# Expert kernel on one core: the fifth batch's routing steps, expert 1's banks and its weight splits in another order

## The chip, the cores and the metric

The kernel runs on one core of a Trainium2 chip. The metric is the device time of one launch in microseconds. All times in this document are microseconds unless another unit stands beside them. TensorE, VectorE (DVE), ScalarE (ACT) and GpSimd (POOL) each work through a queue of their own in order; SyncE (SP) issues most of the DMAs, GpSimd issues the indirect ones (gathers and scatters of rows by index).

## The reference: what is computed

First a linear attention with decay: for 4 batches, 8 heads, 768 positions and 64 features, `state = gamma * state + k v^T` and `y = q state / 8`. The result, seen as 3072 tokens of 512 features, goes through a two-level mixture of experts. `x @ w_group` chooses one of 4 groups, `x @ w_expert[g]` one of 4 experts in it, so each token goes to one of 16 experts:

```python
h  = np.maximum(x[tokens] @ w1[g, e], 0.0)     # 512 -> 1024
ye = h @ w2[g, e]                              # 1024 -> 512
out[tokens] = (g_w * e_w)[:, None] * ye        # two softmax weights
```

The weights and tokens are float32. Each product is made of three 16-bit products: a value is split into a high and a low half (`wh`, `wl` for weights, `xbh`, `xbl` for tokens, `hh`, `hl` for the hidden layer), and high x high, high x low and low x high are summed in PSUM.

## The kernel before

**Attention, steps 0 to 11.** A step `i` handles two blocks of 128 positions for all heads: scores, mask, value products, state, then the logits of the step before (`logits_mm`, L319), the transposes of its output to rows in DRAM (`trans_mm`, L345, into `xd`), and the selection of its 20 logits per token into the PSUM bank `log` (`select_mm`, L332). In some steps the selection is left to the next step (`select_late`).

**Routing, batches 0 to 5.** Two steps make a batch of 4 blocks. `route(b)` is a generator whose pieces are dealt out between the steps (`route_steps`): the choice of group and expert (L384 to L402), which gives a one-hot `oh`; then, after a "wait", the ranks by six matmuls into `log` (L435, L437), the place of each token in its expert's list (L443 to L452, then `places` on GpSimd, L475 to L477), and after one more "wait" the softmax sums and the token's weight (`weights`, L412 to L425 on DVE, L428 to L431 on GpSimd, which cut the weight into three 16-bit pieces). Before the change the sums of all batches but the last are written to the bank `log`. A read or write of that bank waits for those before it, whatever the columns. To put a batch into the lists, DVE makes a mask of list segments (`chosen`, L493) and a one-hot of the places (`marks`, L484), GpSimd multiplies the mask by the pieces (`entries`, L500), and TensorE sums one-hot x product over the blocks (`tally`, L521); DVE adds the sums to the lists (L528).

**The hand-over.** Expert 0 is worked on first. Its first 128 tokens (`ua`) come from the first four batches, so its two layers (`layers`, L839 and L874) run while batches 4 and 5 are still being routed: `first(n)` runs `n` pieces of them (a piece is half of a hidden block, 12 matmuls; eight pieces are the first layer). Expert 0's other tokens (`ub`, up to 108) need the late lists: `late_entries`, `late_marks` (L554) and `late_ids` (L562, L566) make their indices directly, `gather` (L774) fetches the rows. The column count of `ub` (`late_count`, L573 and L574) is loaded into a register of TensorE (`shape`, L806), which cuts its matmuls to the tokens that are there. After that the tally of batches 4 and 5 closes all lists, `order` sorts the experts by size, and `counts` makes their column counts (L638 to L644).

**The experts.** `va` is expert 1, `us[1]` and so on the others in order of size. For each expert eight splits of its weights are made: ACT makes `wh` (L750), DVE makes `wl` (L752), each a piece of 128x1024. A load of 1 MB (`wload`, L724) brings two pieces, and four buffers hold the loads, so that a load waits until the two splits of an older one are done. Tokens are transposed by TensorE (`xtrans`, L792), ACT makes `xbh` (L794) and DVE `xbl` (L817). The hidden layer is made in four blocks (L839), each in a PSUM bank that ACT (`hh`, L844) and DVE (`hl`, L847) read; for `ua` and `ub` three of them are of the tag "big" and the fourth is "tra". Then comes the second layer: L946 for `ub`, L921 and L924 for experts with up to 256 tokens, L874 for full blocks of tokens. While expert `j` runs, `fill(k)` deals out the splits and transposes of expert `j + 1` and the loads of expert `j + 2`. All instructions are issued in the order in which the program writes them, engine by engine. The lines around the loop over `layers(ub)` before the change:

```python
for i, k in enumerate(self.layers(ub)):
    if i in (1, 3, 5, 7, 13, 15):
        low = (1, 3, 5, 7, 13, 15).index(i) + 2
        self.wsplit(va, low, high=False)
        if low % 2:
            self.wload(us[1], low // 2)
    if i in (8, 10):
        self.xtrans(va, ("tra", "sta")[i // 2 - 4], (i // 2 - 4,))
    if i == 11:
        self.counts()
```

Here `i` counts the pieces of `ub`: 0 to 7 are its first layer (after every odd one a hidden block is done), 8 to 15 the eight parts of its second.

Of the kernel before, what the change touches and what calls it, by code (L numbers as in the profile page):

```python
# [22 lines left out]
P = 128  # L23
# [41 lines left out]
BM = 4  # L65
# [41 lines left out]
class Kernel:  # L107
# [251 lines left out]
    def route(self, i):  # L359
# [5 lines left out]
        cst = self.rest  # L365

        def t(name, *shape, dt=F32):
            return rp.tile([P, BM] + list(shape), dt, name=name)[:, 0:n]

        def ps(a, *shape):  # L370
            v = self.log[:, a:a + n * int(np.prod(shape))]
# [4 lines left out]
        L5, d, q, eo = ps(LG, 5, 4), ps(LD, 5, 4), ps(LQ, 5, 4), ps(LO, 4, 4)  # L376
        r1, sm, se, w = ps(LR, NX), ps(LS, 5), ps(LS + 20, 1)[:, :, 0], ps(LS + 24, 1)[:, :, 0]
        sf, pc = self.sf[:, c0:c0 + n], self.pc[:, c0:c0 + n]
        if c0 + n == NCH:
            sm, se, w = t("sms", 5), t("ses"), t("ws")  # L380
        desc = cst[:, C_DESC:C_DESC + 20].rearrange("p (g e) -> p g e", g=5).unsqueeze(1).broadcast_to([P, n, 5, 4])
        oh = self.oh[:, BM - n:BM + 1]
# [685 lines left out]
    def attention(self, extra, beside):  # L1068
# [27 lines left out]
        for i in range(NS2):  # L1096
            last = i == NS2 - 1
            if i == 10:
                self.route_steps(99, True)
                self.spread(3)  # L1100
            if not last:
                self.vprep(i + 1)
            beside(i, -1)
            if i + 1 < NC:
                self.decay_next(i + 1)
            beside(i, 0)
            if i:
                if i > 2:
                    self.outs(i)
                if i > 1:  # L1110
                    scores(i + 1, 0)
                if i % 2 and not last:
                    self.select_late()
                if i in (5, 7, 9):
                    self.tally()
                if i > 2:
                    self.state_out(i, 0)
                if last:
                    self.select_late()
                if i > 1:  # L1120
                    self.state_out(i, 1)
                self.select_late()
                if i % 2 == 0:
                    self.route_steps(99, True)
                if i > 1:
                    scores(i + 1, 1)
            self.load("q", i + 3)
            self.load("v", i + 3)
            if i % 2:
                self.route_steps(99)  # L1130
            beside(i, 2)
            if i:
                self.value_out(i, 0)
            self.value_out(i, 1)
            if i:
                self.state_mm(i, 0)
            self.state_mm(i, 1)
            self.state_copy(i)
            if i == 10:
                self.tally()  # L1140
                beside(i, 5)
            beside(i, 4)
            if i:
                self.logits_mm(i - 1, 1 if last or i % NC == NC - 2 or i + 1 in KEYED else 2)
            self.out_x(i)
            if i < 2:
                scores(i + 1, 0)
                scores(i + 1, 1)
            if i in (4, 6, 8):
                self.spread(i // 2 - 2)  # L1150
            if last:
                self.route_steps(1, True)
            beside(i, 1)
            if not last:
                banks = (self.log, self.sh[0]) if i < 2 else None
                if i == 0:
                    self.keys_mm(1, (0,), banks)
                    self.outs(1)
                    self.state_out(1, 0)
                    self.state_out(1, 1)  # L1160
                    self.keys_mm(1, (1,), banks)
                else:
                    self.keys_mm(i + 1, banks=banks)
                if i == 1:
                    self.outs(2)
                    self.state_out(2, 0)
                self.load("k", i + 4)
            if i:
                late = i + 1 in KEYED or i % NC == NC - 2
                self.trans_mm(i - 1, late=late)  # L1170
                if late:
                    self.late = i - 1
                else:
                    del self.st[i - 1]
            beside(i, 3)
            if last:
                self.route_steps(99)
            if i % 2:
                self.route_steps(99, True)
            if i == 1:  # L1180
                self.const_pieces()
            if last:
                extra(i)
            if i and i % 2 == 0:
                self.steps.append(self.route(i // 2 - 1))
            if not last:
                extra(i)
# [15 lines left out]
    def run(self):  # L1203
        tc, nc = self.tc, self.nc
        with ExitStack() as ctx:
# [80 lines left out]
            last = NS2 - 1  # L1286
            self.logits_mm(last)
            self.trans_mm(last, self.yp)
            nc.gpsimd.memset(self.xg[1], 0.0)
            self.wsplit(va, 1, low=False)  # L1290
            for k in range(8, 16):
                self.wload_part(va, k)
            assert not self.steps
            route = self.route(len(BATCHES) - 1)
            while next(route) != "wait":
                pass
            self.held = []
            first(3)
            self.wsplit(va, 2, low=False)
            late = [self.late_entries(5, self.oh[:, 0:BM, 0:1])]  # L1300
            next(route)
            p, y = self.at
            hot = self.marks(p)
            ent, sel = self.chosen(y)
            late.insert(0, self.late_entries(4, sel[:, :, 1:2]))
            self.spreads.append((hot, self.entries(4, ent, sel)))
            while next(route) != "late":
                pass
            first(2)
            ub["mt"] = self.pairs()  # L1310
            self.late_ids(ub["mt"], (hot, late[0]), (self.hot, late[1]))
            self.gather(ub)
# [7 lines left out]
            self.spreads.append((self.marks(p, self.yp), ent))  # L1320
            nc.vector.scalar_tensor_tensor(*self.held[3])
            self.held = None
            self.late_count()
            self.wsplit(va, 3, low=False)
            self.steps.append(self.order())
            self.route_steps(5)
            for i, k in enumerate(self.first):
                if i == 0:
                    self.shape(ub, 5, 0, self.late_cols)
                    self.wsplit(va, 4, low=False)  # L1330
                if i == 1:
                    self.tally("sta")
                    fin = self.final.rearrange("p e i w -> p (e i) w")
                    self.tokens(fin[:, :, 0], fin[:, :, 1], self.lists)
# [10 lines left out]
            for u in us[1:3]:  # L1345
                self.listed(u)
            self.own_counts()
            for k in range(2):
                self.wsplit(va, k, high=False)
            self.wload(us[1], 0)  # L1350
            ub["wh"], ub["wl"] = ua["wh"], ua["wl"]
            self.gather(us[1])
            for i, k in enumerate(self.layers(ub)):
                if i in (1, 3):
                    self.wsplit(va, 6 + i // 2, low=False)
                if i in (1, 3, 5, 7, 13, 15):
                    low = (1, 3, 5, 7, 13, 15).index(i) + 2
                    self.wsplit(va, low, high=False)
                    if low % 2:
                        self.wload(us[1], low // 2)  # L1360
                if i in (8, 10):
                    self.xtrans(va, ("tra", "sta")[i // 2 - 4], (i // 2 - 4,))
                if i in (9, 10):
                    self.shape(va, 0, i - 9, cols(0, i - 9))
                if i == 11:
                    self.counts()
            self.rp = self.rp2
            self.steps.append(self.items())
# [2 lines left out]
            for j, u in enumerate(us):  # L1371
# [4 lines left out]
                def fill(k):  # L1376
                    if k == 0:
                        self.ytrans(pv)
                    if nx is not None and k in (1, 2):
                        self.shape(nx, (j + 1) % 2, k - 1, cols(j + 1, k - 1))  # L1380
                    if nx is not None and k in KX:
# [64 lines left out]
```

## Time and profile before

| | |
|---|---|
| time, median of 3 runs (lowest, highest) | 412.25 (411.23, 412.8) |
| the profiled execution: its time, its span | 414.38, 412.7 |
| TensorE busy, share of the span | 393.7, 95% |
| DVE, ACT, GpSimd busy | 71%, 54%, 40% |
| mean granted clock of TensorE | 0.992 |
| HBM read, written | 94.18 MB, 13.20 MB |

The span is the time from the first to the last instruction of one profiled execution; 1.68 of its time lie outside the span. Positions such as "at 128.5" are from the span's start. Attention ends and the experts begin at about 108, the loop over the experts begins at 138.3, and TensorE's last matmuls end near 405. In rows of a timeline the columns are: start, duration, engine, line, operation, output and inputs, shape, count, and in brackets the idle time of that engine before the instruction, with what ended it by the profile. That name is inferred from semaphore events.

### The profile page before, as it was taken

Reading aid. Unit: us, or ns where it says so; the run is one execution under the profiler, and the core shown is the slowest. Engines: PE = TensorE matmul, PEld = TensorE weight load, DVE = VectorE, ACT = ScalarE, POOL = GpSimd, SP = SyncE. Lnnn points to the kernel's source line nnn. Section 1 sums busy time; section 2 is a strip of 40 time slices with the busy share of each in tenths; the row PEclk is TensorE's granted clock in tenths of the full one; section 3 lists DMA queues with packets and bytes.
Section 4 is the critical chain, followed back from the end, with each engine's and each line's share of the span. In section 5 each row is a group of like instructions: output and inputs, shape, how many; then the busy total and the mean of one; then the engine's idle time right before and its main releaser. Section 6 shows DMA issues by size and latency. Waiting matters only on the chain.

```text
span 412.7 us, 13870 instructions
## 1 busy us (share of the span) xinstructions
PE 393.7 (95%) x5809; PEld 326.9 (79%) x5841; DVE 293.4 (71%) x483; ACT 223.1 (54%) x340; POOL 165.2 (40%) x172
## 2 busy tenths in 40 slices
PE   9999999989886999999999999999999999999992
PEld 5889989868656979586879797887978879878792
DVE  3575776867769687896767686877869778688620
ACT  2324435534644456555556566666766667667620
POOL 4532767759564205241506051542514415142001
PEclk9999999999999999999999999999999999999998
DMA  7999999975846866777787877879788898797001
GB/s 264 371 335 325 312 352 319 310 273 176 269 153 209 342 228 245 236 262 248 251 252 253 295 249 284 281 273 303 278 306 282 299 317 299 253 341 266 6 35 35
DMA packets 39507, 107.13 MB, mean 260 GB/s; under 512 B 12116, under 2 KB 12244, under 8 KB 32276
## 3 DMA queue, kind: packets, MB, share of 16 engines
q1 hardware_dynamic: 29760, 93.57, 66.0%
q0 software_dynamic: 9536, 12.63, 8.9%
q8 instruction: 47, 0.77, 0.7%
q14 instruction: 16, 0.13, 0.1%
q10 hardware_dynamic: 148, 0.03, 0.0%
HBM read 94.18 MB, written 13.20 MB: 260 GB/s over the span
## 4 chain that ended last, share of the span: by engine, by line
PE 45%; issue 35%; POOL 10%; DVE 6%; ACT 1%; DMA 1%; POOLq 0%; SPq 0%; DVEq 0%; ACTq 0%
PE hps L839 10%; POOL out L998 6%; PE yps L874 6%; PE op L299 5%; PE sh L235 5%; POOL xg L774 4%; PE yps L921 3%; PE op L286 2%; PE stp L261 2%; PE sh L345 2%; PE yps L924 2%; PE tpx L792 1%; PE sh L220 1%; PE log L332 1%; PE yps L946 1%
## 5 line engine op out<-in xcount | busy, mean ns | idle before, releaser
L752 DVE TENSOR_TENSOR wl<-wf,wh 128x1024 bf16<-128x1024 f32 x120 | 145.3, 1220 | 37.7 <-ACT wh L750 36.7
L750 ACT ACTIVATE wh<-wf 128x1024 f16<-128x1024 f32 (+1 forms) x136 | 133.6, 1002 | 0.0
L839 PE MATMUL hps<-xbl,wh 128*128 128x128 f16 (+16 forms) x544 | 128.6, 249 | 0.0
L839 PE MATMUL hps<-xbh,wl 128*128 128x0 bf16 x544 | 125.8, 241 | 0.0
L839 PE MATMUL hps<-xbh,wh 128*128 128x0 bf16 x544 | 125.8, 241 | 0.0
L998 POOL DMA_INDIRECT out<-yo,mt x30 | 39.3, 1309 | 162.9 <-ACT yo L980 125.0
L839 PEld LDWEIGHTS <-wh 128*128 128x128 f16 x1088 | 94.9, 98 | 1.0 <-issue 0.2
L924 PEld LDWEIGHTS <-wh 128*128 128x128 f16 x768 | 47.1, 97 | 22.9
L844 ACT ACTIVATE hh<-hps 128x256 bf16<-128x256 f32 (+16 forms) x68 | 34.2, 503 | 44.2 <-PE hps L839 42.4
L774 POOL DMA_INDIRECT xg<-xd,mt x30 | 51.1, 1704 | 15.2 <-issue 4.9
L839 PEld LDWEIGHTS <-wl 128*128 128x128 bf16 x544 | 53.2, 98 | 0.7
L247 DVE TENSOR_TENSOR pf<-sh,tri 128x512 f32<-128x512 f32 x48 | 30.6, 685 | 24.8 <-PE sh L235 8.6
L794 ACT ACTIVATE xbh<-tpx 128x512 bf16<-128x512 f32 (+14 forms) x32 | 16.7, 523 | 52.4 <-PE tpx L792 52.4
L847 DVE SCALAR_TENSOR_TENSOR hl<-hps,hh 128x216 f16<-128x216 f32 (+15 forms) x64 | 36.7, 574 | 4.9 <-ACT hh L844 4.6
L921 PE MATMUL yps<-wh,hh 128*128 128x512 f16 x96 | 36.4, 379 | 0.0
L921 PE MATMUL yps<-wh,hl 128*128 128x512 f16 x96 | 36.4, 379 | 0.0
L921 PE MATMUL yps<-wl,hh 128*128 128x512 bf16 x96 | 36.3, 378 | 0.0
L817 DVE TENSOR_TENSOR xbl<-tpx,xbh 128x512 f16<-128x512 f32 (+14 forms) x32 | 19.1, 598 | 21.9 <-ACT xbh L794 21.5
L924 PEld LDWEIGHTS <-wl 128*128 128x128 bf16 x384 | 24.2, 97 | 11.4
L192 POOL TENSOR_TENSOR vs<-lv,cst 128x512 f32<-128x512 f32 x24 | 24.6, 1044 | 15.3 <-DMA lv<-qkv 8.8
L924 PE MATMUL yps<-hl,wh 128*128 128x108 f16 (+11 forms) x384 | 29.1, 198 | 0.0
L924 PE MATMUL yps<-hh,wh 128*128 128x0 bf16 x384 | 26.6, 190 | 0.0
(194 smaller groups left out, 601.9 us busy)
## 6 DMA issues: line engine op xcount, KB each, us to landing
wf<-w1p SPq DMA_DIRECT2D x28, 1024.0 KB
wf<-w2p SPq DMA_DIRECT2D x28, 1024.0 KB
lq<-qkv SPq DMA_DIRECT2D x24, 256.0 KB
lk<-qkv SPq DMA_DIRECT2D x24, 256.0 KB
lv<-qkv SPq DMA_DIRECT2D x24, 256.0 KB
xd<-xr SPq DMA_DIRECT2D x22, 256.0 KB
wf<-w1p SPq DMA_DIRECT2D x16, 256.0 KB
wf<-w2p SPq DMA_DIRECT2D x16, 256.0 KB
```

Of the source, the lines that this page charges most:

```text
L192: self.nc.gpsimd.tensor_tensor(o, v, g, ALU.mult)
L247: nc.vector.tensor_tensor(o, sc, tri, ALU.mult)
L750: nc.scalar.activation(u["wh"][i][:, cs], u["wf"][i][:, cs], AF.Copy)
L752: (eng or nc.vector).tensor_tensor(u["wl"][i][:, cs], u["wf"][i][:, cs], u["wh"][i][:, cs], ALU.subtract)
L774: nc.gpsimd.indirect_dma_start(out=xg[0:r, i, :], out_offset=None, in_=self.xd[0:n, :], in_offset=bass.IndirectOffsetOnAxis(ap=mt[0:r, i, ...
L839: nc.tensor.matmul(o, l[:, k, fs], m, start=(n == 0), stop=(n == 11), skip_group_check=True)
L844: nc.scalar.activation(hh[:, f, 0:W], hv[:, :, 0:W], AF.Relu)
L847: nc.vector.scalar_tensor_tensor(*rest)
L874: nc.tensor.matmul(ps[0:r, :], l[:, k, ts], m[k], start=(n == 0), stop=(n == 23))
L921: nc.tensor.matmul(big, h[:, k, 0:P], w[k], start=(n == 0), stop=(n == 23))
L924: nc.tensor.matmul(o, w[k][:, d * P:d * P + P], m, start=(n == 0 and d == 0), stop=(n == 23), skip_group_check=True,)
L998: s = nc.gpsimd.indirect_dma_start(out=self.out, out_offset=bass.IndirectOffsetOnAxis(ap=mt[0:r, i, 0:1].bitcast(U32), axis=0), in_=yo[0:r ...
```

## The change

It does six things. The selection of step 8's logits in step 10 goes behind the value and state matmuls. Batch 4's sums go to SBUF, as the last batch's do, with two buffers for `ex` and `go`. Batch 4's ranks are read in step 11 at once, its mask, one-hot and late product are made before the choice of the last batch, its sums after that choice, and its list product after the last batch's places. Of expert 0's first layer 2, 3 and 3 pieces are dealt out instead of 3, 2 and 3; the late column count and its register load move (the count ahead, the load behind). Expert 1's token transposes go to the banks "sta" and "big". Its `wl` splits and the loads of the next expert are dealt out over more pieces, the last two splits and the last load in expert 1's own first layer, and the column counts come after piece 15, not 11.

```diff
-            return rp.tile([P, BM] + list(shape), dt, name=name)[:, 0:n]
+            bufs = 2 if name in ("ex", "go") else 1
+            return rp.tile([P, BM] + list(shape), dt, name=name, bufs=bufs)[:, 0:n]
...
-        if c0 + n == NCH:
+        if c0 + n > NCH - 2 * BM + 1:
             sm, se, w = t("sms", 5), t("ses"), t("ws")
...
                 if i > 1:
                     self.state_out(i, 1)
-                self.select_late()
+                if i < NS2 - 2:
+                    self.select_late()
...
             if i == 10:
+                self.select_late()
                 self.tally()
...
             if last:
                 self.route_steps(1, True)
+                self.route_steps(99)
...
-            if last:
-                self.route_steps(99)
-            if i % 2:
+            if i % 2 and not last:
                 self.route_steps(99, True)
...
             self.trans_mm(last, self.yp)
-            nc.gpsimd.memset(self.xg[1], 0.0)
+            p, y = self.at
+            ent, sel = self.chosen(y)
+            hot = self.marks(p)
+            late = [self.late_entries(4, sel[:, :, 1:2])]
             self.wsplit(va, 1, low=False)
             for k in range(8, 16):
                 self.wload_part(va, k)
-            assert not self.steps
             route = self.route(len(BATCHES) - 1)
             while next(route) != "wait":
                 pass
             self.held = []
-            first(3)
+            self.route_steps(99, True)
+            assert not self.steps
+            first(2)
             self.wsplit(va, 2, low=False)
-            late = [self.late_entries(5, self.oh[:, 0:BM, 0:1])]
+            late.append(self.late_entries(5, self.oh[:, 0:BM, 0:1]))
             next(route)
-            p, y = self.at
-            hot = self.marks(p)
-            ent, sel = self.chosen(y)
-            late.insert(0, self.late_entries(4, sel[:, :, 1:2]))
-            self.spreads.append((hot, self.entries(4, ent, sel)))
             while next(route) != "late":
                 pass
-            first(2)
+            self.spreads.append((hot, self.entries(4, ent, sel)))
+            self.late_count()
+            first(3)
             ub["mt"] = self.pairs()
             self.late_ids(ub["mt"], (hot, late[0]), (self.hot, late[1]))
             self.gather(ub)
...
-            self.late_count()
+            nc.gpsimd.memset(self.xg[1], 0.0)
             self.wsplit(va, 3, low=False)
...
                 if i == 0:
-                    self.shape(ub, 5, 0, self.late_cols)
                     self.wsplit(va, 4, low=False)
                 if i == 1:
+                    self.shape(ub, 5, 0, self.late_cols)
                     self.tally("sta")
...
-            for k in range(2):
-                self.wsplit(va, k, high=False)
-            self.wload(us[1], 0)
+            self.wsplit(va, 0, high=False)
...
-                if i in (1, 3, 5, 7, 13, 15):
-                    low = (1, 3, 5, 7, 13, 15).index(i) + 2
+                if i in (3, 7, 9, 11, 13):
+                    low = (3, 7, 9, 11, 13).index(i) + 1
                     self.wsplit(va, low, high=False)
                     if low % 2:
                         self.wload(us[1], low // 2)
                 if i in (8, 10):
-                    self.xtrans(va, ("tra", "sta")[i // 2 - 4], (i // 2 - 4,))
+                    self.xtrans(va, ("sta", "big")[i // 2 - 4], (i // 2 - 4,))
...
-                if i == 11:
+                if i == 15:
                     self.counts()
...
+                    if j == 0 and k in (1, 2):
+                        self.wsplit(u, 5 + k, high=False)
+                        if k == 2:
+                            self.wload(nx, 3)
```

## Rows read from the trace of the kernel before

**Rows 1.** Busy time by stage: stretch, length, busy time (instructions) per engine, clock, DMA, GB/s.

```profile
113.00:120.00 7.00, 4.89 (x53) 3.30 (x55) 5.30 (x22) 3.60 (x5) 5.24 (x10) 1.00 0.69 242
...
132.20:138.30 6.10, 6.10 (x94) 6.01 (x97) 3.79 (x8) 1.13 (x2) 2.57 (x3) 0.72 1.01 410
...
160.00:200.00 40.00, 40.00 (x295) 29.14 (x298) 33.81 (x43) 23.06 (x30) 13.20 (x9) 1.00 0.77 257
```

**Rows 2.** TensorE's waits, 92 to 160: line, waited for, total, times, longest.

```profile
PE log L332 <- DVE ecols L463: 0.9, 1, 0.9
PE log L562 <- DVE lhot L554: 0.8, 1, 0.8
PE log L332 <- DVE wt L425: 0.7, 1, 0.7
PE log L435 <- ACT ex L408: 0.3, 1, 0.3
```

**Rows 3.** Timeline of DVE, 124 to 160.

```profile
125.20 2.34 DVE L752 TENSOR_TENSOR wl<-wf,wh 128x1024 bf16<-128x1024 f32 x2
...
131.75 0.36 DVE L847 SCALAR_TENSOR_TENSOR hl<-hps,hh 128x216 f16<-128x216 f32 x1
...
133.60 0.69 DVE L817 TENSOR_TENSOR xbl<-tpx,xbh 128x512 f16<-128x512 f32 x1 [0.36 <-issue]
...
136.66 0.41 DVE L638 TENSOR_TENSOR eqc<-eq,cnt 128x256 f32<-128x256 f32 x1
```

**Rows 4.** Timeline of TensorE, 126 to 142.

```profile
132.16 0.77 PE L792 MATMUL tpx<-ident,xg 128*128 128x128 f32 x4 [3.62 <-DVE hl L847]
```

**Rows 5.** Timeline of TensorE, 114 to 140.

```profile
118.65 0.38 PE L874 MATMUL yps<-wh,hh 128*128 128x512 f16 x1 [1.42 <-DVE gt L606]
...
119.94 0.72 PE L521 MATMUL tally<-yT,hot 128*128 128x160 bf16 x8
```

**Rows 6.** Timeline of ACT, 120 to 160.

```profile
127.28 0.83 ACT L844 ACTIVATE hh<-hps 128x216 bf16<-128x216 f32 x2
...
155.49 1.05 ACT L750 ACTIVATE wh<-wf 128x1024 f16<-128x1024 f32 x1
```

**Rows 7.** Timeline of DVE, 107 to 120.

```profile
106.84 0.23 DVE L412 TENSOR_REDUCE log<-ex 128x20 f32<-128x80 f32 x1
...
108.00 0.18 DVE L425 RECIPROCAL wt<-log 128x4 f32<-128x4 f32 x1
108.96 0.24 DVE L384 TENSOR_REDUCE m<-log 128x20 f32<-128x80 f32 x1 [0.78 <-PE log L332]
...
110.55 0.22 DVE L402 TENSOR_TENSOR oh<-log,go 128x64 bf16<-128x64 f32 x1
110.69 0.68 DVE L484 TENSOR_TENSOR hot<-rest,place 128x512 bf16<-128x512 f32 x1
...
112.56 1.07 DVE L554 SCALAR_TENSOR_TENSOR lhot<-rest,sf 128x512 bf16<-128x512 f32 x1 [0.18 <-DMA wf<-w2p]
...
117.56 0.14 DVE L574 TENSOR_SCALAR lcols<-fcols 1x1 int32<-1x1 f32 x1
```

**Rows 8.** Timeline of GpSimd, 107 to 120.

```profile
108.27 0.24 POOL L428 TENSOR_SCALAR pc<-wt 128x4 bf16<-128x4 f32 x1 [0.42 <-DVE wt L425]
...
109.20 0.21 POOL L431 TENSOR_TENSOR pc<-wt,pc 128x4 bf16<-128x4 f32 x1
...
111.81 1.27 POOL L500 TENSOR_TENSOR yT<-yT,pc 128x640 bf16<-128x640 bf16 x1
113.17 0.56 POOL L475 TENSOR_SCALAR tile<-sf 128x4 f32<-128x4 f32 x1
...
115.21 1.15 POOL L774 DMA_INDIRECT xg<-xd,mt  x1 [0.88 <-DMA wf<-w2p]
...
118.20 1.54 POOL L500 TENSOR_TENSOR yT<-yT,pc 128x640 bf16<-128x640 bf16 x1
```

**Rows 9.** Timeline of SP's DMA issues, 120 to 160.

```profile
133.37 7.32 SPq L724 DMA_DIRECT2D wf<-w2p  x2
```

## The prediction

> **What bounds the kernel now.** I read in this order: the busy time by stage, TensorE's waits, the timeline of each engine in the stretch that holds them. By stage, TensorE is busy for all of 160 to 200 at full clock [rows 1]; its waits from 160 on are none, so the expert loop is TensorE's own work, and this change leaves that work as it is (the same matmuls, transposes and splits in another order). What can be won lies before 160, in the list of TensorE's waits from 92 on: 0.9, 0.8, 0.7 and 0.3 us around the routing of the last two batches [rows 2], and two longer ones that the timeline shows in their place: 3.62 us before the transposes of expert 1's tokens (L792) [rows 4], 1.42 us before a second-layer matmul (L874) [rows 5]. They sum to 7.7 us. They cost more or less than they look. After the 3.62 us the granted clock is 0.72 on the mean over 132.2 to 138.3 [rows 1]: TensorE was busy for all 6.10 us, so 0.28 x 6.10 = 1.71 us went to the half-rate clock (1.2 of 2.4 GHz). And the small waits lie on a chain that runs through GpSimd, so that taking one away can open the next.
>
> **Part 1: expert 1's banks and the order of its splits** (the loop over layers(ub)). Before, DVE's queue there is two splits (125.20, 2.34 us), then in turn one hl (0.36 us) and one more split (1.20 us) [rows 3]: the fourth hl starts at 131.75 and ends at 132.11, when three more splits stood ahead of it. The first transposes of expert 1 go into the bank "tra", which holds the fourth hidden block until that hl has read it, so TensorE stands from 128.54 to 132.16 [rows 4]. The change sends the first transposes to "sta" and the second to "big". "sta" was last used by the tally (matmuls at 119.94 [rows 5], its sum on DVE right behind), "big" by the hidden block whose hl is the first in the queue. So the 3.62 us go, and with them the half-rate clock, 1.71 us.
>
> What is late next is DVE, since expert 1's first matmul needs both xl parts. New queue from 125.20: split 0, hl, hl, split 1, hl, hl, split 2, xl, split 3, xl. That is 4 x 1.20 + 4 x 0.36 + 2 x 0.69 = 7.6 us, to 132.8. hh, which hl waits for, is done for all four blocks by 128.11 [rows 6], so nothing holds the last two hl. TensorE is there at 128.54 + 6.10 x 0.72 = 132.9 (the busy time of the stretch at full clock). Both meet within 0.2 us: expert 1's matmuls start at 132.9, not at 138.29 or so: 5.4 us. If DVE starts late by x, x is lost; I allow 0 to 0.9.
>
> Of what is moved: the column counts (four instructions from 136.66, about 1.3 us [rows 3]) now come after splits 4 and 5, so at 132.8 + 2.4 + 1.3 = 136.5; TensorE wants them after expert 1's second hidden block, 4.8 us into it, at 137.7; cover 1.2 us. A register load from a fresh value held TensorE from 117.70 (the end of L574 [rows 7]) to 118.65 [rows 5], 0.95 us, so 0.25 us of cover is left and I charge nothing, 0.5 at worst. The last two splits (2 x 1.23) now stand in expert 1's own first layer; they are wanted in its second layer 9 us later, beside a DVE that is not full there. The fourth load of the next expert is issued after the last split and behind the first load of the expert after; the ACT split that reads it starts at 155.49 [rows 6], so at 150 in the new time. It is issued at about 143.3; 6.7 us for it, a charge of nothing in the sum and a rival below.
>
> **Part 2: the fifth batch.** Sums in SBUF for batch 4 too: the last selection (L332) no longer waits for the sums in the logit bank, 0.67 us [rows 2]. The late column count: the 1.4 us before L874 are TensorE's register load of it; DVE makes it at 117.56 behind all else [rows 7]; in the new order it is made right after the last one-hot, some 4 us earlier, and that wait goes. But the tally comes next on TensorE, right at 119.94, and it needs the last list product of GpSimd, 118.20 + 1.54 = 119.74 [rows 8]. So what counts is GpSimd's chain. New: selection ends 0.67 us earlier; the seven instructions of the choice from L384 (108.96) to the end of L402 (110.77) take 1.81, so the one-hot is there at 110.1 [rows 7]. Ahead of L384 batch 4's mask and one-hot (of which L484, 0.68 us, is the long one) take the place of its sums (106.84 to 108.18, 1.34 us), so L384 still waits for TensorE alone; behind the choice those sums now stand: reciprocal at 111.4. GpSimd: the four piece instructions 108.27 to 109.41 = 1.14 us, to 112.6; a small product 0.3; the three of the places, 0.84 when free and 1.16 beside DVE (L475 took 0.56 beside the last one-hot, 0.24 is the four-column rate of L428 [rows 8]), to 113.9; the list product of batch 4 with 1.27 to 1.54, to 115.2 to 115.5; the gather start, 115.21 before, now 115.3 to 116.2 (0.1 to the 0.88 us of idle that stood before it), 1.15 us long; the four pieces of batch 5, 1.14 to 1.73; the last product, 1.27 to 1.54. End: 118.9 to 120.6 against 119.74. I take the middle, 119.75: part 2 is worth **0**, bounds -0.85 to +0.9. TensorE has 11.02 - 0.26 - 0.84 - 1.42 = 8.5 us of work from the selection's end (108.92) to the tally; from 108.25, with 0.8 before the ranks (it has two half blocks there, not three) and 0.2 before the late ids, it comes to the tally at 117.8 and stands for some 1.9 us: the removed waits come back as one. The two buffers for ex and go only let batch 5 write them before batch 4's sums have read theirs. The memset of xg moves behind the last product (0.95 us of GpSimd, while it waited 1.8 us for the list before): nothing.
>
> The rule that speaks against this part is in the Trainium skill, SBUF — State Buffer, "Who interferes with whom": VectorE and GpSimd share one pair of ports as an exclusive lock, and the one that comes second stands until the first is done. L475 shows it: 0.56 us, ending at 113.73, 0.10 after the one-hot of DVE (112.56 + 1.07 [rows 7]). By it more of GpSimd's work would now fall on DVE's instructions with two SBUF operands, the moved sums among them, and the time would be that of the port rival below.
>
> **Part 3: the selection in step 10** goes behind the value matmuls; 0.9 us of TensorE's wait for the sums of batch 3 go [rows 2]. Behind it stands the gather of the first expert's tokens, which sits on GpSimd behind two scalings of v that do not move; its rows had just landed when TensorE transposed them. I take 0 to 0.6, value 0.1, and what comes of it runs into the chain of part 2.
>
> **The sum**, against the profiled execution: 414.38 - 3.62 - 1.71 (part 1) - 0 (part 2) - 0.1 (part 3) = 408.95, 5.4 less. The runs shown have a median of 412.25, 2.1 below the profiled one; I take the difference over unchanged: 412.25 - 5.4 = **406.8**. The likeliest case alone: best 405.3 (0.85 of part 2 and 0.6 of part 3 more), worst 408.6 (0.9 of each of parts 1 and 2 less).
>
> **Rivals.** (a) The clock. The half rate is lost again elsewhere: 1.9 us at the tally, 0.8 before the ranks and 0.2 before the late ids lie within ten us. For: it fell after an idle piece of 3.62 us. Against: 113 to 120, with the waits of 0.8 and 1.4, kept clock 1.00 [rows 1]. Or the timed runs did not all have it, and the median loses less. Either way 1.71 us: 408.5. 18%.
>
> (b) The port. DVE's sums of batch 5 stand behind GpSimd's product of batch 4 (1.27 us), the last marks behind its pieces; the last product ends 0.7 later: 407.5. 10%.
>
> (c) The change does not do what it says: the transposes in "sta" go, but the matmuls behind them wait for hl or xl as long, because DVE is full from 125.20 to 133.24 before [rows 3] and has the same work after. For: DVE has no pause there that would take up a shift. Against: four of its splits move behind the last xl. It needs DVE to be 3.5 us later than summed: 410.3 to 412.3. 7%.
>
> (d) The slower one: the next expert's weights. Loads 1, 2 and 3 are issued 1.8, 1.9 and 2.9 us later than now (load 2 at 133.37, load 3 at the end of that 7.32 us, 140.35 [rows 9]), while ACT wants them 5.4 us earlier. ACT runs in order, so a split without its weights holds the next hidden block. It decides from 6.7 us between issue and landing of load 3. All the rows say is that load 3 was there at 155.49, at most 15.1 us after its issue. At that bound ACT stands 15.1 - 6.7 = 8.4 us and TensorE behind it: 406.8 + 8.4 = 415.2. Against: DMA moved 410 GB/s in 132.2 to 138.3 [rows 1], at which 1 MB takes 2.6 us, and two loads 5.1. 5%.
>
> **How the numbers follow.** Likeliest 60%, (a) 18, (b) 10, (c) 7, (d) 5. A measurement of this kernel tells 0.5%, 2.1 us, from no change: faster means below 410.2. Likeliest, (a) and (b) are faster: 88%. (c) is mostly the same: 7%. (d) is slower: 5%. Range 405.3 to 410.0: from the best end of the likeliest to past (a) with 0.9 and 0.6 of the unknown costs on it; what is left out is (c), (d) and a little at both ends.
>
> **What would show it.** Right: no wait of some 3.6 us before L792, granted clock 1.00 from 128 to 140, expert 1's first matmul near 133; the waits at L332, L562 and before L874 gone or small and a new one of 1 to 2 us at the tally (L521), which starts between 119 and 120.7; the fourth hl of ub near 129. Wrong: another wait at L839 behind xl, waits of TensorE in 140 to 160, ACT's splits waiting for DMA, or a half-rate stretch after the tally. If the tally comes 1 us or more earlier, part 2 was worth something and GpSimd was not its bound.

## The result and the profile after

The changed kernel takes 406.98 (median of 4 runs, 405.39 to 407.63) where the kernel before takes 411.85 in the same comparison (411.23 to 412.8): ratio 0.9874, 95% interval 0.9837 to 0.9911. That is 4.9 less, 1.3%, and by the bound of 0.5% it is faster. The forecast was 406.8, 5.4 less than 412.25. Two later comparisons of the changed kernel (e8, e11) gave 0.9862 [0.9822, 0.9901] and 0.9878 [0.9843, 0.9913].

The profiled execution took 407.63, its span is 405.9. Lines of the code behind the first edit are one higher than before (L792 is now L793, L500 is L501). The first view of after is the list of TensorE's waits, which answers to [rows 2]; its columns are the same.

```profile
PE log L436 <- ACT ex L409: 1.0, 1, 1.0
PE tally L522 <- POOL yT L501: 0.9, 1, 0.9
PE op L286 <- DVE xt L311: 0.9, 2, 0.7
PE log L522 <- POOL yT L501: 0.4, 1, 0.4
PE yps L875 <- DVE hl L1320: 0.3, 1, 0.3
PE log L563 <- DVE lcols L575: 0.2, 1, 0.2
```

The 3.62 before L792 [rows 4] is not in it, nor the 0.9 and the 0.7 at L332, the 0.8 before the late ids and the 1.42 before L874 [rows 2, 5]. In their place stand 0.9 at the tally and 1.0 before the ranks; the waits at L286 (0.7 of the 0.9) and at the step-10 tally (0.4) are new.

The busy time by stage of after answers to [rows 1]; the first line is a stretch that is not in them.

```profile
99.80:103.40 3.60, 3.60 (x34) 3.27 (x36) 1.91 (x7) 1.18 (x2) 0.56 (x1) 0.53 0.84 225
...
132.20:138.30 6.10, 6.10 (x69) 6.03 (x69) 5.12 (x11) 3.79 (x6) 5.44 (x3) 1.00 0.99 388
160.00:200.00 40.00, 40.00 (x300) 29.35 (x302) 32.15 (x39) 22.79 (x30) 12.49 (x9) 1.00 0.75 256
```

Behind the hand-over the clock is now 1.00, where it was 0.72. But this one execution has a stretch of attention at 0.53 (it takes 0.47 x 3.60 = 1.7), which neither of the two later profiles of the same kernel has. TensorE's timeline shows the hand-over, against [rows 4, 5]:

```profile
118.00 0.44 PE L522 MATMUL tally<-yT,hot 128*128 128x160 bf16 x4
119.33 0.44 PE L522 MATMUL tally<-yT,hot 128*128 128x160 bf16 x4 [0.89 <-POOL yT L501]
...
127.16 0.62 PE L793 MATMUL tpx<-ident,xg 128*128 128x128 f32 x4
...
128.61 0.55 PE L793 MATMUL tpx<-ident,xg 108*128 108x108 f32 x4
...
131.60 0.26 PE L840 MATMUL hps<-xbl,wh 128*128 128x236 f16 x1
```

No bracket stands behind L793: the transposes wait for nothing. The tally, eight matmuls in one piece before, now does four, waits, and does four. Expert 1's first matmul is at 131.60 (before 138.12). DVE's timeline shows why, against [rows 3], and three of its instructions in the routing:

```profile
106.60 1.63 DVE L485 TENSOR_TENSOR hot<-rest,place 128x512 bf16<-128x512 f32 x1
...
113.91 1.08 DVE L421 TENSOR_SCALAR u<-sms 128x4 f32<-128x4 f32 x1
...
118.03 1.53 DVE L607 TENSOR_TENSOR gt<-key 128x256 f32<-128x256 f32 x1
...
124.31 1.20 DVE L753 TENSOR_TENSOR wl<-wf,wh 128x1024 bf16<-128x1024 f32 x1
...
127.16 0.65 DVE L848 SCALAR_TENSOR_TENSOR hl<-hps,hh 128x216 f16<-128x216 f32 x2
...
130.60 0.59 DVE L818 TENSOR_TENSOR xbl<-tpx,xbh 128x432 f16<-128x432 f32 x1
131.12 2.34 DVE L753 TENSOR_TENSOR wl<-wf,wh 128x1024 bf16<-128x1024 f32 x2
133.39 0.41 DVE L639 TENSOR_TENSOR eqc<-eq,cnt 128x256 f32<-128x256 f32 x1
```

The fourth `hl` ends at 127.81, 4.3 earlier than before (132.11), and the second `xbl` at 131.19, 0.4 ahead of the matmul that reads it. GpSimd's timeline, against [rows 8]:

```profile
112.01 0.66 POOL L432 TENSOR_TENSOR pc<-wt,pc 128x4 bf16<-128x4 f32 x1
...
113.69 1.27 POOL L501 TENSOR_TENSOR yT<-yT,pc 128x640 bf16<-128x640 bf16 x1
115.15 1.16 POOL L775 DMA_INDIRECT xg<-xd,mt  x1 [0.19 <-DVE u L421]
...
118.01 1.26 POOL L501 TENSOR_TENSOR yT<-yT,pc 128x640 bf16<-128x640 bf16 x1
```

The gather stands where it stood (115.21 before) and the last product ends at 119.27 (119.74 before): GpSimd's chain sets the tally.

**Three lengths that hold in every trace.** They don't depend on where an execution has got to when it reaches them, so they say what each part is worth. W: the sum of TensorE's idle pieces of more than 0.12 that begin between 84 and 104. R: from the start of the last selection's wait (or of the selection, where it waits for nothing) to the fifth matmul of the tally. H: from there to expert 1's first matmul. From that matmul to TensorE's last it is 266.55 or 266.56 in eleven of the thirteen traces, 266.68 in e2 and 268.98 in e1, so almost nothing behind the hand-over differs.

| kernel | median (runs) | ratio to before [95%] | W | R | H |
|---|---|---|---|---|---|
| before | 412.25 (3) | | 1.22 | 12.57 | 17.91 |
| changed | 406.98 (4) | 0.9874 [0.9837, 0.9911] | 1.27* | 11.88 | 12.27 |
| e1, banks alone | 409.16 (6) | 0.9911 [0.988, 0.9942] | 1.24 | 12.59 | 14.36 |
| e2, splits alone | 409.24 (9) | 0.9921 [0.9894, 0.9947] | 1.22 | 12.58 | 13.05 |
| e3, part 1 alone | 408.06 (6) | 0.9896 [0.9865, 0.9928] | 1.22 | 12.59 | 13.45 |
| e4, all but part 1 | 412.97 (12) | 0.999 [0.9967, 1.0013] | 2.25 | 11.86 | 18.01 |
| e5, early sums | 406.2 (6) | 0.9845 [0.9803, 0.9887] | 2.39 | 11.24 | 12.30 |
| e6, step 10 put back | 405.59 (6) | 0.9834 [0.9793, 0.9875] | 1.39 | 11.87 | 12.29 |
| e7, product on DVE | 407.28 (6) | 0.9863 [0.9822, 0.9904] | 1.93 | 11.67 | 12.59 |
| e8, changed again | 406.72 (6) | 0.9862 [0.9822, 0.9901] | 2.07 | 11.88 | 12.33 |
| e9, e5 and e6 | 406.91 (6) | 0.9831 [0.9797, 0.9864] | 1.21 | 11.22 | 13.34 |
| e10, e6 again | 407.19 (6) | 0.9835 [0.9803, 0.9867] | 1.35 | 11.87 | 13.34 |
| e11, changed again | 409.03 (6) | 0.9878 [0.9843, 0.9913] | 2.18 | 11.87 | 13.33 |

\* with the stretch at half the clock, in which TensorE came late enough not to wait for the gather. e1 to e4, e5 to e8 and e9 to e11 ran on one chip each; the kernel before had medians of 412.86, 412.21 and 414.3 there, so ratios are compared across chips, and times only within one. Intervals of differences below are 95%, from the runs of one chip (Welch's t).

### The profile page after: what moved, and what is told of

Its sections match the earlier page's. It is cut to its first block, busy times and chain, and to the rows that moved or that the text cites. A ratio compares the mean times of both kernels' runs of the same rounds, so it can differ in the third digit from the quotient of the medians.

```text
span 405.9 us, 13868 instructions
## 1 busy us (share of the span) xinstructions
PE 391.5 (96%) x5809; PEld 326.0 (80%) x5841; DVE 295.5 (73%) x483; ACT 223.4 (55%) x340; POOL 169.1 (42%) x172
## 4 chain that ended last, share of the span: by engine, by line
PE 46%; issue 35%; POOL 12%; DVE 3%; ACT 1%; DMA 1%; POOLq 0%; SPq 0%; ACTq 0%; DVEq 0%
PE hps L840 11%; POOL out L999 6%; PE yps L875 6%; PE op L299 5%; PE sh L235 4%; POOL xg L775 4%; PE yps L922 3%; PE op L286 2%; PE sh L345 2%; PE stp L261 2%; PE yps L925 2%; PE tpx L793 1%; PE sh L220 1%; PE sh L319 1%; PE log L332 1%
## 5 line engine op out<-in xcount | busy, mean ns | idle before, releaser
L753 DVE TENSOR_TENSOR wl<-wf,wh 128x1024 bf16<-128x1024 f32 x120 | 145.3, 1220 | 36.6 <-ACT wh L751 36.3
L840 PE MATMUL hps<-xbl,wh 128*128 128x128 f16 (+16 forms) x544 | 128.6, 249 | 0.0
L840 PE MATMUL hps<-xbh,wl 128*128 128x0 bf16 x544 | 125.8, 241 | 0.0
L840 PE MATMUL hps<-xbh,wh 128*128 128x0 bf16 x544 | 125.8, 241 | 0.0
L840 PEld LDWEIGHTS <-wh 128*128 128x128 f16 x1088 | 94.9, 98 | 1.0 <-issue 0.2
L775 POOL DMA_INDIRECT xg<-xd,mt x30 | 54.2, 1807 | 13.1 <-PE tpx L793 4.5
L840 PEld LDWEIGHTS <-wl 128*128 128x128 bf16 x544 | 53.2, 98 | 0.7
```

The lines of the kernel that those rows point to most:

```text
L753: (eng or nc.vector).tensor_tensor(u["wl"][i][:, cs], u["wf"][i][:, cs], u["wh"][i][:, cs], ALU.subtract)
L775: nc.gpsimd.indirect_dma_start(out=xg[0:r, i, :], out_offset=None, in_=self.xd[0:n, :], in_offset=bass.IndirectOffsetOnAxis(ap=mt[0:r, i, ...
L840: nc.tensor.matmul(o, l[:, k, fs], m, start=(n == 0), stop=(n == 11), skip_group_check=True)
```

## The experiments

**e1: the banks alone**, in the kernel before.

```diff
-                    self.xtrans(va, ("tra", "sta")[i // 2 - 4], (i // 2 - 4,))
+                    self.xtrans(va, ("sta", "big")[i // 2 - 4], (i // 2 - 4,))
```

> The kernel before with the two bank tags of expert 1's transposes changed alone. Theory (the wait is the bank that the fourth hl holds, and DVE's xl is what is late next): transposes near 128.5, no wait of 3.6 us there, no half-rate clock; but xl stands behind six splits in DVE's queue (xl parts end near 134.6), so expert 1's first matmul starts near 134.6 instead of 138.3: 3.7 us less, 408.2. Rival (the banks are the whole of part 1): first matmul near 132.9, 5.4 us less, 406.5. Rival (the splits' order is what counts): within 1 us of before.

Measured 409.16, 3.7 less than before, as expected (408.2 was the figure for a kernel before of 411.85). The wait is gone, in TensorE's timeline and two rows of DVE's of e1:

```profile
126.04 0.63 PE L792 MATMUL tpx<-ident,xg 128*128 128x128 f32 x4
...
132.15 0.26 PE L946 MATMUL yps<-hl,wh 128*128 128x108 f16 x2 [0.46 <-issue]
132.24 0.26 PE L839 MATMUL hps<-xbl,wh 128*128 128x236 f16 x1
...
132.92 0.26 PE L839 MATMUL hps<-xbh,wl 128*128 128x0 bf16 x1 [0.33 <-issue]
```

```profile
129.70 1.20 DVE L752 TENSOR_TENSOR wl<-wf,wh 128x1024 bf16<-128x1024 f32 x1
130.83 1.19 DVE L817 TENSOR_TENSOR xbl<-tpx,xbh 128x512 f16<-128x512 f32 x2
```

The `xbl` parts stand behind six splits and end at 132.02; expert 1's first matmul, which reads them, is at 132.24. That fits the expected mechanism, that `xbl` is what is late next. The profile hides it, since TensorE has pauses of 0.37, 0.38 and 0.46 before that matmul which it puts down to nothing; without them it would have stood for `xbl` nearly as long. H is 0.9 longer than with both halves (e3). In this profile the granted clock was at one half (1.2 of 2.4 GHz) from 133.63 to 137.04, with no longer idle piece than these in the hand-over before it. That costs 0.5 x 3.41 = 1.7 and, with the 0.33, makes most of the 2.4 by which the 268.98 of this trace is longer.

**e2: the order of splits and counts alone**, with the old banks.

```diff
-            for k in range(2):
-                self.wsplit(va, k, high=False)
-            self.wload(us[1], 0)
+            self.wsplit(va, 0, high=False)
...
-                if i in (1, 3, 5, 7, 13, 15):
-                    low = (1, 3, 5, 7, 13, 15).index(i) + 2
+                if i in (3, 7, 9, 11, 13):
+                    low = (3, 7, 9, 11, 13).index(i) + 1
...
-                if i == 11:
+                if i == 15:
                     self.counts()
...
+                    if j == 0 and k in (1, 2):
+                        self.wsplit(u, 5 + k, high=False)
+                        if k == 2:
+                            self.wload(nx, 3)
```

> The kernel before with the order of expert 1's splits, of the loads and of the column counts changed alone; the transposes stay in tra and sta. Theory: the fourth hl now ends near 129.2 instead of 132.1, so the wait at the first transposes shrinks from 3.62 to some 0.6 us, too short for the half-rate clock; first matmul of expert 1 near 133.4, 4.8 us less, 407.0. Rival (the banks are the whole): within 1 us of before.

Measured 409.24, 3.6 less than before, where 4.8 was expected. The wait shrinks to 0.54, in TensorE's timeline of e2:

```profile
126.55 0.66 PE L792 MATMUL tpx<-ident,xg 128*128 128x128 f32 x4 [0.54 <-DVE hl L847]
```

With the fourth `hl` early enough, the old bank costs half a microsecond. Each half alone removes most of the same wait, which is why their gains (3.7 and 3.6) don't add up.

**e3: part 1**, the edits of e1 and e2 together in the kernel before.

```diff
-            for k in range(2):
-                self.wsplit(va, k, high=False)
-            self.wload(us[1], 0)
+            self.wsplit(va, 0, high=False)
...
-                    self.xtrans(va, ("tra", "sta")[i // 2 - 4], (i // 2 - 4,))
+                    self.xtrans(va, ("sta", "big")[i // 2 - 4], (i // 2 - 4,))
...
```

> The kernel before with both of these, the routing left as it was. Theory (prediction): 5.4 us less, 406.4 against 411.85; first matmul of expert 1 near 132.9. Rival (parts 2 and 3 are worth something by themselves): less than 5 us of the change's gain here, 407.5 or more.

Measured 408.06, ratio 0.9896: 4.4 less on the mean (3.5 to 5.3). H falls from 17.91 to 13.45, that is 4.5, with two pauses of 0.39 and 0.41 before L946 in it; the changed kernel's own 12.27 has none. On the mean e1 is slower than e3 by 1.0 (-0.2 to 2.1) and e2 by 0.8 (-0.4 to 2.0): neither is told from it.

**e4: everything but part 1**, the changed kernel with the old banks and splits.

```diff
-            self.wsplit(va, 0, high=False)
+            for k in range(2):
+                self.wsplit(va, k, high=False)
+            self.wload(us[1], 0)
...
-                    self.xtrans(va, ("sta", "big")[i // 2 - 4], (i // 2 - 4,))
+                    self.xtrans(va, ("tra", "sta")[i // 2 - 4], (i // 2 - 4,))
...
```

> The changed kernel with banks, splits, loads and counts put back: the routing parts alone. Theory (prediction): the removed waits come back at the tally, 0 to 0.9 us less, 411.0 to 411.9, with the wait of 3.6 us and the half-rate clock still there. Rival: the removed waits stay away, 3 us less, 408.8.

Measured 412.97, ratio 0.999 [0.9967, 1.0013]: the routing's edits alone are worth nothing that can be measured. The wait before the transposes and the half-rate clock behind it are back, in TensorE's timeline and the busy time by stage of e4:

```profile
130.99 0.63 PE L793 MATMUL tpx<-ident,xg 128*128 128x128 f32 x4 [3.38 <-issue]
```

```profile
132.20:138.30 6.10, 6.10 (x91) 6.06 (x90) 3.65 (x8) 1.12 (x3) 2.77 (x3) 0.72 0.95 377
```

The profile names "issue" here, but DVE's fourth `hl`, which holds the old bank, ended at 130.89, 0.10 before the transposes, as in the kernel before (132.11 and 132.16).

The clock can be followed in the timed runs too. Their mean granted clock is 0.9903 in the kernel before (42 runs, 0.985 to 0.993), 0.9914 in e4 (12 runs), and 0.9950 in the ten experiments whose kernel has part 1 or half of it (63 runs, 0.989 to 0.997). 0.0047 of 405 is 1.9: the 1.71 belongs to the timed runs as a group, not to one profile.

**e5: batch 4's sums earlier**, in step 11, its list product ahead of the last ranks (and the first layer in 3, 2 and 3 pieces again).

```diff
-            if i % 2 and not last:
+            if i % 2:
                 self.route_steps(99, True)
...
-            self.route_steps(99, True)
             assert not self.steps
-            first(2)
+            self.spreads.append((hot, self.entries(4, ent, sel)))
+            first(3)
...
-            self.spreads.append((hot, self.entries(4, ent, sel)))
             self.late_count()
-            first(3)
+            first(2)
```

> The changed kernel with batch 4's sums back in step 11 (in SBUF), its list product ahead of the last ranks, and 3, 2 and 3 pieces of the first layer. Theory (GpSimd's chain to the tally bounds the routing): the chain is relieved of 1.1 us of pieces and the product leaves the way of the gather, so the tally comes 1.0 to 1.6 us earlier against the last selection, the waits of 1.05 and 0.89 us go to under 0.5 each; 1.0 to 1.6 us less than the changed kernel. Rival (TensorE's own work, or DVE, bounds it): same as the changed kernel within 0.5 us.

TensorE's waits in e5:

```profile
PE tpx L793 <- DMA xg<-xd,mt: 1.1, 1, 1.1
PE log L436 <- ACT ex L409: 1.0, 1, 1.0
...
PE log L563 <- DVE fcols L574: 0.5, 1, 0.5
PE tally L522 <- POOL yT L501: 0.4, 1, 0.4
```

With the product out of the chain's way the wait at the tally halves and R falls by 0.64: GpSimd's chain was the bound. The 1.0 before the ranks did not move; it ends with ACT's `ex`, behind the choice. Measured 406.2 beside e8's 406.72: 0.8 less on the mean (-0.3 to 1.9), which by itself is not told from nothing; 1.0 to 1.6 was expected.

**e6: step 8's selection back in its old place.**

```diff
-                if i < NS2 - 2:
-                    self.select_late()
+                self.select_late()
...
-                self.select_late()
                 self.tally()
```

> The changed kernel with the selection of step 10 put back behind the state matmuls. Theory (prediction): a wait of some 0.9 us before L332 comes back near 91, and costs 0 to 0.6 us at the end, since the gather of expert 0's tokens stands behind. Rival: the 0.9 us come back whole.

Measured 405.59, 1.1 less on the mean than the changed kernel (0.2 to 2.0), where 0 to 0.6 more was expected. Rows of e6 (first) and of e8, the changed kernel again (second), merged timeline of GpSimd, SP and TensorE:

```profile
91.06 0.62 PE L332 MATMUL log<-rest,ls 128*128 128x20 f32 x4 [0.89 <-DVE ecols L464]
...
96.87 1.28 POOL L775 DMA_INDIRECT xg<-xd,mt  x1 [0.32 <-DVE mt L534]
...
97.59 0.81 SPq L356 DMA_DIRECT2D xd<-xr  x2
...
98.46 1.95 SPq L739 DMA_DIRECT2D wf<-w1p  x4
...
101.93 0.66 PE L793 MATMUL tpx<-ident,xg 128*128 128x128 f32 x4 [0.18 <-DMA xg<-xd,mt]
```

```profile
96.75 1.28 POOL L775 DMA_INDIRECT xg<-xd,mt  x1 [0.18 <-issue]
96.92 0.81 SPq L356 DMA_DIRECT2D xd<-xr  x2
...
97.33 0.40 PE L286 MATMUL op<-lq,V 64*64 64x128 f32 x2 [0.69 <-DVE xt L311]
...
97.78 1.92 SPq L739 DMA_DIRECT2D wf<-w1p  x4
...
102.43 0.66 PE L793 MATMUL tpx<-ident,xg 128*128 128x128 f32 x4 [0.79 <-DMA xg<-xd,mt]
```

With the selection moved, the 0.89 at L332 is gone and comes back as 0.39 at the step-10 tally, 0.69 at L286 and 0.79 at the transposes of the gathered rows. The gather starts where it did (14.1 behind the same L235 matmul in e7 and e11, 14.2 in the kernel before), and the transposes start 5.68 behind it instead of 5.06. In the seven traces with the old place this distance is 4.89 to 5.06 and the next weight load is issued 1.58 to 1.60 behind the gather; in the six with the new place it is 5.55 to 6.42 and 1.03 to 1.04. (The 6.42 is the profile with half the clock there.) The gather's own landing is in twelve of the traces: 4.84 to 5.01 behind its issue with the old place, 5.51 to 5.96 with the new one. So its rows do come later. But two things moved up behind it: the load, and the two stores of token rows ahead of that load (`xd<-xr`), which come 0.17 behind the gather instead of 0.71 to 0.73. That these transfers meet the gather's rows is argued from the distances, and which of the two it is no run tells; a kernel that moves the load alone was not tried.

**e7: the last list product on DVE instead of GpSimd.**

```diff
-        self.nc.gpsimd.tensor_tensor(ent, sel.unsqueeze(3).broadcast_to([P, BM, NL, PIECES]), pc, ALU.mult)
+        eng = self.nc.vector if b == 5 else self.nc.gpsimd
+        eng.tensor_tensor(ent, sel.unsqueeze(3).broadcast_to([P, BM, NL, PIECES]), pc, ALU.mult)
```

> The changed kernel with the list product of batch 5 on DVE instead of GpSimd. Theory (GpSimd is the tally's bound): the product takes some 0.85 instead of 1.26 us and DVE's L607 is no longer held beside it; the tally comes 0.4 us earlier, the wait before it falls to about 0.5; time 0.4 us less. Rival (DVE is as full): the expert order after it comes later, the splits of expert 1 with it, and expert 1 begins up to 0.8 us later.

DVE's timeline of e7:

```profile
113.86 1.08 DVE L421 TENSOR_SCALAR u<-sms 128x4 f32<-128x4 f32 x1
...
117.61 0.82 DVE L502 TENSOR_TENSOR yT<-yT,pc 128x640 bf16<-128x640 bf16 x1 [1.02 <-POOL pc L432]
118.35 0.68 DVE L485 TENSOR_TENSOR hot<-rest,place 128x512 bf16<-128x512 f32 x1
...
119.83 0.42 DVE L608 TENSOR_TENSOR gt<-key 128x256 f32<-128x256 f32 x1
```

The product takes 0.82 instead of 1.26, but the last one-hot now stands behind it, so the tally gains 0.2 (R 11.67) of the 0.4 expected, and the time nothing (+0.2, -0.7 to +1.1). L608 takes 0.42 here; it took 1.53 beside GpSimd's product.

**e8: the changed kernel again**, no edit.

> The changed kernel itself beside the others. Every theory: 5.2 us below before; the granted clock of its runs like that of e3_part1 (0.993 to 0.997).

Measured 406.72. Its profile has no half-rate stretch from attention to the end of the experts.

**e9: the edits of e5 and e6 together; e10: e6's again; e11: the changed kernel again**, on one chip.

The core of e9's edit:

```diff
-                if i < NS2 - 2:
-                    self.select_late()
+                self.select_late()
...
-            self.route_steps(99, True)
             assert not self.steps
-            first(2)
+            self.spreads.append((hot, self.entries(4, ent, sel)))
+            first(3)
...
```

> The changed kernel with step 8's selection back in its old place in step 10 and batch 4's sums and list product ahead of the last ranks (the two edits that were tried one by one before). By the theory that the waits only change their place: in the profile of the changed kernel run again, TensorE's waits from 84 to 120 are 0.39, 0.69, 0.20, 0.79, 1.05, 0.18, 0.30 and 0.89 us, 4.49 in sum; with both edits I expect 0.89, 0.12, 0.20, 0.18, 1.02, 0.46 and 0.45, 3.32 in sum, so 1.2 us less: 405.5, with the wait before L332 back at 0.9 and those before L286 and L793 gone. By the rival, that the two edits help each other (an earlier gather frees GpSimd for the chain to the tally), the waits before the ranks and the tally shrink as well and the time is below 404.8. By the other rival, that neither edit does anything and the runs of 405.6 to 406.7 are one time, it is 406.4.

> The changed kernel with only step 8's selection back in its old place, once more, beside the kernel with both edits. By the theory that the waits only change their place, TensorE's waits from 84 to 120 sum to 3.8 us as in its first profile, against 4.49 in the changed kernel's: 406.0, which is 0.7 below the changed kernel's 406.72. By the rival, that the place of this selection makes no difference, 406.7.

> The changed kernel a second time on the chip of the two others, for their comparison: 406.7, between 405.9 and 407.6, as it has been. If its profile shows a stretch at the half-rate clock in attention again, that belongs to the kernel; if it shows none, as the last one did, it belongs to the single execution.

Measured 406.91, 407.19 and 409.03. The old place of the selection is better in both pairs (e6 against e8, e10 against e11): by 1.4 on the mean of the two differences, interval 0.8 to 2.0; the traces hold 0.7 to 0.8 of it as waits, the rest is not placed. e5's edits on top bring 0.2 here (-0.6 to 1.1), and 0.5 (-0.1 to 1.1) over both chips, though R is shorter by 0.65 in both traces: not settled. e9 is 1.9 (0.8 to 3.1) faster than the changed kernel, where 1.2 was expected, and e6, e9 and e10 have the lowest ratios of all (0.983); the one sure part of that is one edit put back.

On this chip H is 13.33 or 13.34 in all three kernels, on that of e5 to e8 it is 12.3 to 12.6, for the same instructions. In the three traces TensorE has a pause of 0.44 ahead of L840 at "issue" and then 0.2 to 0.3 ahead of `xbl`; what holds it at the first one the profile does not show.

## Why the prediction was right

The total came out within 0.2 of the forecast, by one large term that was right and two small ones that were wrong in opposite directions. That these two cancel is luck, and so is some of the rest: the gain was 4.9 where 5.4 was forecast, from a median before of 411.85 and not 412.25.

**Part 1 (5.4): right.** H is shorter by 5.3 to 5.6 in the traces of changed kernels without pauses and by 4.5 to 4.6 in those with them; the timed gain of e3, whose trace has two of the pauses, is 4.4 (3.5 to 5.3), and of the whole changed kernel on the mean of e8 and e11 it is 5.4 (4.6 to 6.2). A small reading was off: expert 1's first matmul was at 138.12 before, not 138.29, so the positions give 5.2 and the sum's two terms 5.33. Both sub-terms show: the wait is gone, and the clock of all timed runs rose by about what 1.7 of half rate makes (1.9). Expert 1's first matmul at 131.60 is 1.3 earlier than the 132.9 of the sum; 0.9 of that is the tally's, which part 2 had put at no change. DVE and TensorE were to meet within 0.2: they nearly do, `xbl` is 0.4 to 0.7 early in five traces (after, e5 to e8), and in e9 to e11, with the pause, TensorE waits 0.2 to 0.3 for it. The counts were done at 134.66, not 136.5, and cost nothing.

**Part 2 (0, bounds -0.85 to +0.9): mis-sized, inside its bounds.** R is shorter by 0.70 in the six traces with these edits as they are (after, e4, e6, e8, e10, e11). The tally came at 119.33 (119 to 120.7 expected), the gather at 115.15 (115.3 expected at the earliest), the product's end at 119.27 (118.9 expected at the earliest, 119.75 taken). TensorE was to stand 1.9 at the tally, 0.8 before the ranks and 0.2 before the late ids; it stands 0.89, 1.05, 0.18 and 0.30 before L875. Where the 0.70 is: this trace is 0.20 ahead at the start of R, so the product ends 0.27 sooner than before instead of at the same time (its gather found the indices ready since 113.44 and stood idle for 0.19, not for up to 0.88); the tally follows it by 0.06 instead of 0.20; and its first four matmuls, 0.28, now run ahead of the wait, which the sum had left out. The mechanism, that GpSimd's chain takes over from the removed waits, is what e5 shows.

**Part 3 (0.1 of gain, bounds 0 to 0.6): wrong in sign.** The step that failed is "I take 0 to 0.6". It had named the gather behind the moved selection and that its rows had just landed, so that TensorE would wait for them; but it took the gather's landing as fixed. It moved, by 0.6 and 0.8 in the two pairs (e6 and e8, e10 and e11): W is 0.9 longer (2.16 on the mean of e4, e5, e7, e8 and e11, 1.26 on that of the seven with the old place). The stores and the weight load behind the gather come 0.55 sooner there, which is the likely cause and not a shown one. And nothing was won ahead of the gather to begin with: the removed 0.89, with 0.12 at L286, came back as 0.39 at the step-10 tally and 0.69 at L286 (e6 against e8). Part 2's -0.7 and this +0.9 cancel, which is e4's ratio of 0.999.

**The rivals.** (a), the clock lost again elsewhere: seen in one profile of the changed kernel (0.53 in 99.8 to 103.4) and one of e1, not in the timed runs as a whole. (b), the port: the lock is there, its price of 0.7 at the last product is not. L421, a step of the last batch's sums on DVE, took 1.08 from 113.91 to 114.98 while GpSimd's product ran from 113.69 to 114.96, and 0.16 in the batch before it; L607 took 1.53 beside the other product and 0.42 in e7 (there L608), where that product is on DVE. This is the lock of the Trainium skill (SBUF — State Buffer, "Who interferes with whom"), by which the one that comes second stands until the first is done, and the trace agrees: L421 ended 0.02 behind the product. The sums were ready at 115.47, when GpSimd had its gather until 116.31, so nothing waited for them. Two other holds did fall on the chain. DVE's L485 took 1.63 beside a split on GpSimd (L753, from 106.52), and 0.68 in batch 5, so the choice began 0.18 behind the end of the selection and not 0.04: it did not "wait for TensorE alone". GpSimd's L432 took 0.66, ending 0.07 behind DVE's L555, and 0.24 in batch 5. The bounds of part 2 had room for them. (c), the wait moving to `hl` or `xbl`: 0.2 to 0.3 in three traces, not 3.5. (Of DVE's splits two moved behind the last `xbl`, not four: six stood ahead of it before, four do now.) (d), the loads: SP's timeline of after has the load, and ACT's the split that reads it.

```profile
142.03 0.33 SPq L725 DMA_DIRECT2D wf<-w2p  x1
```

```profile
149.34 1.06 ACT L751 ACTIVATE wh<-wf 128x1024 f16<-128x1024 f32 x1 [0.27 <-DMA wf<-w2p]
```

The load of the last two pieces, issued at 142.03, landed at 149.31, 7.28 later, where the prediction had 6.7 of cover. So ACT did wait for DMA, 0.27, which was named as a sign of being wrong; TensorE waited for nothing.

## What to carry to other kernels

Where an engine stands for several microseconds at a hand-over, look for what the waiting step's buffer shares with a queue in order: here either half of the edit (another bank, or the reader moved up in its queue) took away most of the wait, and what the second half added, 0.8 to 1.0 on the mean, is not told from nothing. Price the clock with the wait, and check it in the mean granted clock of all timed runs, not in one profile. And where a wait is moved ahead of a transfer, the transfer's landing is not a constant: ask which other transfers are let go earlier by the same move, and test them one at a time.

## What was not expected of the hardware

The granted clock was at one half in attention (after, 99.87 to 103.29) and at the hand-over (e1, 133.63 to 137.04), with idle pieces of 0.38, 0.69 and 0.20 and of 0.37, 0.38, 0.46 and 0.33 before it; the changed kernel's two later profiles, with the same pieces, kept 1.00. The same instructions took 1.0 longer at the hand-over (H 13.33 against 12.3) in the profiles from two chips, with a pause that the profile puts down to no other engine.
